# A hand-written instruction order: a transpose, one exponential and one weight step moved, and seven more matmul steps whose result is never read

## The chip, the cores and the metric

The kernel runs on one core of a Trainium2 chip. Its engines work side by side: TensorE (PE, with its weight loads as PEld), VectorE (DVE), ScalarE (ACT), GpSimd (POOL), and SyncE (SP), which here only issues DMAs. The metric is the device time of one execution in microseconds (us), as the median of three runs. Less is better.

## What is computed

Two attention steps with 32 packed rows per head, then a dense layer with a SoLU activation and a layer norm. Cut to its core:

```python
# q, k, v: (8, 8, 576, 64); p: (8, 8, 32, 64); w_in: (512, 1024); w_out: (1024, 512)
p_packed = sm_attn(p, k, v)                 # softmax(scale * p k^T) v, 32 rows per head
out = sm_attn(q, p_packed, p_packed)        # 576 rows per head
x = out.transpose(0, 2, 1, 3).reshape(4608, 512)
h = x @ w_in
solu = h * softmax(h)
ln = (solu - mean) / sqrt(var + 1e-06) * g_ln
return ln @ w_out
```

## The kernel before

For each of the 8 batches three flows prepare the data. `k0` to `k7` (`pack`) turn k, form the scores with the packed rows, take their maximum and exponential, and multiply by v: the result is the packed tile `ppT`. `q0` to `q7` (`unpack`) turn q, form the scores against `ppT`, take the softmax, and split the result into two halves of 16 bits, `a_h` and `a_l`. `z0` to `z7` (`make_z`) multiply `ppT` by w_in into Z, also split in a high and a low half. Then 36 token tiles `t0` to `t35` of 128 rows (`token_tile`) follow: 12 matmuls at each of two 512-wide halves give h (line 630), DVE, ACT and POOL make the activation, a DMA turns it, and 24 matmuls multiply by w_out (line 690).

Other flows prepare the weights: `W0` to `W3` convert w_in, `O0` to `O3` convert w_out, `C0` to `C7` scale it, `g` turns g_ln on PE (line 186) and copies it to SBUF on ACT (line 188), and `H` makes 16-bit halves of w_in for later batches: per chunk, ACT makes the high half (line 342) and DVE the low half (line 344). One step of `W0` is a pass of ACT over the chunk (line 229), a shift on DVE (line 231), and a second pass of ACT (line 242, the low bits).

`Z` and `X` compute nothing that is read. `Z` is 39 matmuls at the start. `X` (`keep_clock`) issues two matmuls of 384 columns into the spare PSUM tile each time it is called; only its columns 128 to 511 are written, and `g` uses columns 0 to 7.

Nothing here is ordered by a planner. Each flow is a Python generator, and the string `ORDER` says which flow makes its next step (line 733, `next(flows[name], None)`). Each engine takes its instructions in that order and starts one when what it waits for is there. A step that stands earlier in `ORDER` is therefore earlier on each engine's queue that it touches, and an instruction that waits holds up all that follow it on that engine. PSUM has three `h` buffers, in turn used by the transposes (lines 209, 372, 378), the first scores (line 402), the transposes of the exponentials (line 443), Z (line 576) and h.

In batch 0 the flow `k0` goes: transposes of k (372, 378), copies, scores for r = 0 (402, PE), maximum (407, DVE), exponential (410, ACT), the same three for r = 1, then the transposes of both exponentials (443, PE), of which the first needs r = 0 alone and the rest r = 1 too, then the product with v (453, PE).

Of the kernel before, what the change touches and what calls it, by code (L numbers as in the profile page):

```python
# [49 lines left out]
def packed_attention_solu_kernel(ctx: ExitStack, tc: tile.TileContext, q: bass.AP, k: bass.AP, v: bass.AP, p: bass.AP, w_in: bass.AP, w_out: bass.AP, g_ln: bass.AP, out: bass.AP):  # L50
    nc = tc.nc
    B, H, S, D = q.shape
# [67 lines left out]
        yield  # L120

    def keep_clock():
        for _ in range(4):
            for _ in range(2):
                nc.tensor.matmul(spare[:, P:], lhsT=ones, rhs=ones.unsqueeze(1).broadcast_to([P, DM // P - 1, P]), start=True, stop=True)
            yield
# [481 lines left out]
    def token_tile(i, dst, b, c):  # L608
# [77 lines left out]
        for o0 in range(0, DM, wide):  # L686
# [73 lines left out]
```

## Time and profile before

| what | before |
|---|---|
| time, median of 3 runs | 391.14 us (388.96 to 392.26) |
| the profiled execution's own time | 389.22 us |
| its span, first to last instruction | 387.4 us |
| mean granted TensorE clock | 1.000 |
| PE busy | 377.0 us (97%) |
| DVE, ACT, POOL busy | 292.5, 256.7, 245.9 us |

The span is 1.82 us shorter than the time of the same execution. The profiled execution lies near the fastest of the three runs and 1.92 us under their median. A matmul's end is modelled, so that the busy time of PE overlaps from one instruction to the next; where one group of matmuls starts after another is the safer reading.

### The profile page before, as it was taken

The page shows a single profiled execution, that of the slowest core. Times are in us where ns is not written, and L with a number is a line of the kernel's source. Part 1 is how long each engine was busy: PE and PEld are TensorE (multiplying, and loading weights), DVE is VectorE, ACT ScalarE, POOL GpSimd, SP SyncE. Part 2 cuts the span into 40 slices and gives each one's busy share as a digit, 9 for nine tenths or more (in the row PEclk, how much of TensorE's full clock was granted, in tenths as well). Part 3 has the DMA queues.
Part 4 walks back from the last instruction along what each step waited for, and adds up shares of the span by engine and source line. Part 5 has one row for each costly group of instructions (what it writes and reads, how often), then busy time and mean ns, then how long its engine had stood idle before and what let it go on. Part 6 is the DMA issues. An engine that isn't in the chain of part 4 may idle for free.

```text
span 387.4 us, 8803 instructions
## 1 busy us (share of the span) xinstructions
PE 377.0 (97%) x3380; PEld 194.6 (50%) x3380; DVE 292.5 (76%) x472; ACT 256.7 (66%) x447; POOL 245.9 (63%) x410
## 2 busy tenths in 40 slices
PE   6978999999999999999999999999999999999996
PEld 6856555444545444544454455444455444444445
DVE  2576889999997987778797589977777868477541
ACT  2386799795878677945757757754648559466640
POOL 2664589888438987764555477885456757853660
PEclk9999999999999999999999999999999999999999
DMA  8999993899899899999799878991631533344461
GB/s 304 389 374 358 205 215 57 211 187 180 153 237 171 199 197 180 173 182 219 160 191 144 215 142 175 183 179 47 159 81 37 129 91 98 85 104 104 92 162 55
DMA packets 213866, 66.11 MB, mean 171 GB/s; under 512 B 194744, under 2 KB 207808, under 8 KB 213312
## 3 DMA queue, kind: packets, MB, share of 16 engines
q1 hardware_dynamic: 213824, 65.56, 74.8%
q8 instruction: 26, 0.43, 0.5%
q14 instruction: 16, 0.13, 0.1%
HBM read 37.23 MB, written 9.44 MB: 120 GB/s over the span
## 4 chain that ended last, share of the span: by engine, by line
PE 90%; ACT 4%; DVE 2%; POOL 2%; issue 1%; DMA 1%; POOLq 0%
PE po L690 39%; PE h L630 24%; PE h L690 5%; PE h L372 4%; PE pa L453 3%; PE h L402 3%; PE h L570 2%; PE h L522 2%; PE po L117 2%; PE h L443 2%; POOL a_l L538 1%; PE po L119 1%; PE h L209 1%; PE h L576 1%; ACT e L410 1%; ACT e L672 1%
## 5 line engine op out<-in xcount | busy, mean ns | idle before, releaser
L690 PE MATMUL po<-wch,yT 128*128 128x512 f16 x512 | 160.1, 379 | 0.0
L690 PEld LDWEIGHTS <-yT 128*128 128x128 f16 x888 | 85.9, 98 | 99.2 <-issue 4.5
L690 PE MATMUL po<-wcl,yT 128*128 128x512 f16 x256 | 97.0, 379 | 0.0
L655 DVE SCALAR_TENSOR_TENSOR u<-e,s_row,h 128x1024 f32<-128x1024 f32 x36 | 45.8, 1271 | 16.5 <-ACT e L651 11.1
L633 DVE TENSOR_REDUCE nm<-h 128x1 f32<-128x1024 f32 x36 | 43.6, 1213 | 9.5 <-PE h L630 9.0
L666 DVE SCALAR_TENSOR_TENSOR yhl<-u,negmu,yhl 128x1024 f16<-128x1024 f32 x36 | 46.5, 1292 | 4.0 <-ACT yhl L664 3.9
L630 PE MATMUL h<-zh,a_h 128*128 128x512 f16 (+1 forms) x160 | 47.8, 380 | 0.0
L630 PE MATMUL h<-zl,a_h 128*128 128x512 f16 (+1 forms) x160 | 47.7, 380 | 0.0
L651 ACT ACTIVATE e<-h,nmc,z_scale 128x1024 f32<-128x1024 f32 x36 | 43.2, 1201 | 2.2 <-PE h L630 0.8
L630 PEld LDWEIGHTS <-a_h 128*128 128x128 f16 (+1 forms) x320 | 27.7, 100 | 33.0 <-issue 3.8
L664 ACT ACTIVATE yhl<-u,negmu 128x1024 f16<-128x1024 f32 x36 | 41.1, 1144 | 0.7
L672 ACT ACTIVATE e<-u,negmu 128x1024 f32<-128x1024 f32 x36 | 41.0, 1138 | 0.0
L638 ACT ACTIVATE nmc<-nm,z_scale 128x1 f32<-128x1 f32 x33 | 9.7, 293 | 44.2 <-DVE nm L633 44.1
L641 POOL TENSOR_SCALAR bound<-nm,z_scale 128x1 f32<-128x1 f32 x33 | 13.8, 419 | 36.7 <-DVE nm L633 35.3
L630 PE MATMUL h<-zl,a_l 128*128 128x512 f16 (+1 forms) x80 | 30.4, 380 | 0.4 <-POOL a_l L538 0.4
L630 PE MATMUL h<-zh,a_l 128*128 128x512 f16 (+1 forms) x80 | 30.3, 379 | 0.0
L679 POOL TENSOR_SCALAR c_row<-sq,s_eps 128x1 f32<-128x1 f32 x36 | 11.7, 326 | 28.5 <-ACT e L672 25.5
L698 DVE TENSOR_SCALAR o_sb<-po,c_row,inv 128x512 f32<-128x512 f32 x18 | 14.6, 810 | 15.8 <-PE po L690 6.9
L680 POOL TENSOR_TENSOR c_row<-c_row,neg_half 128x1 f32<-128x1 f32 x36 | 22.7, 630 | 3.0
L659 ACT ACTIVATE negmu<-su 128x1 f32<-128x1 f32 x36 | 7.2, 199 | 26.1 <-DVE u L655 26.1
L630 PEld LDWEIGHTS <-a_l 128*128 128x128 f16 (+1 forms) x160 | 14.8, 100 | 18.0 <-POOL a_l L538 1.2
L506 POOL TENSOR_TENSOR a<-a,sm 128x576 f32<-128x576 f32 x16 | 20.3, 1275 | 5.2 <-DVE sm L504 4.4
(171 smaller groups left out, 700.2 us busy)
## 6 DMA issues: line engine op xcount, KB each, us to landing
out_dram<-o_sb SPq DMA_DIRECT2D x35, 256.0 KB, 2.4
v_sb<-in_v_dram SPq DMA_DIRECT2D x8, 1024.0 KB, 7.6
raw<-in_k_dram SPq DMA_DIRECT2D x24, 288.0 KB, 4.6
raw<-in_q_dram SPq DMA_DIRECT2D x96, 72.0 KB, 2.5
zh<-in_moe_w_in_dram SPq DMA_DIRECT2D x2, 1024.0 KB, 8.4
zl<-in_moe_w_in_dram SPq DMA_DIRECT2D x2, 1024.0 KB, 9.6
raw<-in_k_dram SPq DMA_DIRECT2D x2, 1024.0 KB, 11.9
raw<-in_moe_w_out_dram SPq DMA_DIRECT2D x2, 1024.0 KB, 8.3
```

What stands on the lines that cost most here:

```text
L372: nc.tensor.matmul(pt[64 * r:64 * r + 64, g * MAIN + c * P:g * MAIN + (c + 1) * P], lhsT=rows[:, c, 2 * (g0 + g) + r], rhs=ident, start=Tr ...
L506: EN(nc, SOFT_BY[2 * b + 1]).tensor_tensor(out=w2, in0=w2, in1=sm.unsqueeze(2).broadcast_to([P, NB, J]), op=ALU.mult)
L630: nc.tensor.matmul(dst_[:, cols], lhsT=lhsT, rhs=z[:, r, cols], start=bool(first), stop=bool(last))
L633: nc.vector.tensor_reduce(out=nm, in_=h, axis=AX.X, op=ALU.max, negate=True)
L651: nc.scalar.activation(e, h, AF.Exp, bias=nmc, scale=sc[:, 1:], accum_out=se)
L655: nc.vector.scalar_tensor_tensor(out=u, in0=e, scalar=s_row, in1=h, op0=ALU.mult, op1=ALU.mult, accum_out=su)
L664: nc.scalar.activation(yhl[:, 0], u, AF.Identity, bias=negmu)
L666: nc.vector.scalar_tensor_tensor(out=yhl[:, 1], in0=u, scalar=negmu, in1=yhl[:, 0], op0=ALU.add, op1=ALU.subtract)
L672: nc.scalar.activation(e, u, AF.Square, bias=negmu, accum_out=sq)
L680: nc.gpsimd.tensor_tensor(out=c_row, in0=c_row, in1=neg_half, op=ALU.pow)
L690: nc.tensor.matmul(po[:, cols], lhsT=yT[:, a, c], rhs=w[:, c, cols], start=c == 0 and t == 0, stop=c == NFC - 1 and t == 2)
L698: nc.vector.tensor_scalar(out=o_sb[:, cols], in0=po[:, cols], scalar1=c_row, scalar2=inv, op0=ALU.mult, op1=ALU.mult)
```

## The change

Four edits, of which one also changes a function and the others only `ORDER`:

- `g` makes its first step (the transpose on PE) some 15 steps later. Its second step stays.
- `k0` makes its exponential for r = 0, its scores for r = 1 and their maximum before `W0` makes its steps, where before `W0`'s first three steps stood ahead of the exponential. The exponential for r = 1 still stands behind both ACT passes of `W0`.
- `X` is called 11 times in place of 4. Two of the new calls stand before the transposes of batch 0's exponentials; five stand between Z of batch 0 and the first token tile.
- One step of `H` (the low half of one w_in chunk, on DVE) is made seven steps later, behind the last step of batch 1's Z.

```diff
     def keep_clock():
-        for _ in range(4):
+        for _ in range(11):
             for _ in range(2):
                 nc.tensor.matmul(spare[:, P:], lhsT=ones, ...)
             yield
```

The first place in the string, cut out of its line on both sides (the same stretch before and now):

```diff
-X X k0 k0 lo1 W0 lq0 g W0 W0 k0 k0 W0 k0 p k0 k0 O0 W3 p lv0
+X X k0 k0 lo1 k0 k0 k0 W0 lq0 W0 W0 W0 p X X k0 k0 O0 W3 g p lv0
```

**PE, batch 0's first attention step.** Here `h` is a PSUM buffer, `e` in line 209 is p's rows, `e_112` the exponentials.

```order
 L378 MATMUL h<-ident,raw 128x128 x2
 L125 MATMUL po<-ones 128x384 x4
-L402 MATMUL h<-kT,pT 32x288 x8
+L402 MATMUL h<-kT,pT 32x288 x16
+L209 MATMUL h<-ident,e 64x128 x8
+L125 MATMUL po<-ones 128x384 x4
 L186 MATMUL po<-ident,g_raw 128x8
-L402 MATMUL h<-kT,pT 32x288 x8
-L209 MATMUL h<-ident,e 64x128 x8
 L443 MATMUL h<-ident,e_112 128x128 x8
```

The transpose of g no longer stands between the scores of r = 0 and r = 1, and four new unread matmuls stand right ahead of the transposes of the exponentials.

**ACT, the same place.** The rows named L229 and L242 on `zh` are the two passes of `W0`; L410 are the two exponentials.

```order
 L215 ACTIVATE pT<-h 128x512
 L380 COPY kT<-h 128x2x2x64
+L410 ACTIVATE e_112,ssum<-h,nmx 128x576
 L229 ACTIVATE e<-zh 128x1024
-L410 ACTIVATE e_112,ssum<-h,nmx 128x576
 L242 ACTIVATE u<-zh,one_up 128x1024
 L410 ACTIVATE e_112,ssum<-h,nmx 128x576
```

Only the first exponential has changed places with the first pass of `W0`; the second exponential still follows both passes.

**PE, from batch 0's Z to the first token tile** (line 630 is the first matmul of `t0`; line 372 and 378 are transposes of the next k and q, line 402 the scores of batch 1).

```order
 L576 MATMUL h<-w_in_sb,ppT 32x512 x4
+L125 MATMUL po<-ones 128x384 x2
 L372 MATMUL h<-ident,raw 64x128 x16
 L277 MATMUL pa<-ssq,ones_f 128x8
+L125 MATMUL po<-ones 128x384 x2
 L576 MATMUL h<-w_in_sb,ppT 32x512 x4
 L372 MATMUL h<-ident,raw 64x128 x16
 L576 MATMUL h<-w_in_sb,ppT 32x512 x4
+L125 MATMUL po<-ones 128x384 x2
 L378 MATMUL h<-ident,raw 128x128 x2
+L125 MATMUL po<-ones 128x384 x2
 L402 MATMUL h<-kT,pT 32x288 x8
```

Four pairs of unread matmuls are new here; a fifth pair stands after the transposes that follow, directly ahead of the first matmul of `t0`.

**DVE, batch 1's Z.** Line 344 is the step of `H`; line 586 is the low half of Z, line 666 a low half in a token tile.

```order
+L666 SCALAR_TENSOR_TENSOR yhl<-u,negmu,yhl 128x1024
+L586 SCALAR_TENSOR_TENSOR zl<-h,z_scale,zl 128x1024
 L344 SCALAR_TENSOR_TENSOR w_in_sb<-w_in_sb,s_w,w_hi 128x1024
-L666 SCALAR_TENSOR_TENSOR yhl<-u,negmu,yhl 128x1024
-L586 SCALAR_TENSOR_TENSOR zl<-h,z_scale,zl 128x1024
 L385 STREAM_TRANSPOSE kT<-raw 128x576
```

The low half of w_in now follows the other two in place of leading them. POOL's and SP's orders are the same in both kernels.

## Rows read from the trace of the kernel before

**Rows 1.** The page's busy times by engine: busy us, share, instructions.
```profile
PE 377.0 (97%) x3380; PEld 194.6 (50%) x3380; DVE 292.5 (76%) x472; ACT 256.7 (66%) x447; POOL 245.9 (63%) x410
```

**Rows 2.** Waits of PE: who waited for whom, us in total, times, longest.
```profile
PE h L209 <- DMA e<-in_p_dram: 3.0, 1, 3.0
...
PE pa L453 <- issue: 0.7, 1, 0.7
...
PE h L630 <- POOL a_l L538: 0.4, 1, 0.4
PE pa L277 <- DVE wsq L326: 0.3, 1, 0.3
```

**Rows 3.** Stretches: length, busy PE, PEld, DVE, ACT, POOL; PEclk, DMA share, GB/s.
```profile
25.00:28.00 3.00, 1.60 (x19) 1.44 (x21) 1.77 (x4) 2.55 (x6) 2.92 (x2) 1.00 1.12 355
40.00:45.00 5.00, 5.00 (x62) 2.86 (x60) 4.90 (x12) 3.13 (x5) 3.46 (x3) 1.00 1.00 257
45.00:50.00 5.00, 4.42 (x58) 2.56 (x58) 3.86 (x13) 4.41 (x10) 3.17 (x3) 1.00 1.07 170
50.00:55.00 5.00, 5.00 (x86) 3.79 (x80) 4.33 (x8) 5.00 (x9) 4.18 (x4) 1.00 1.08 271
200.00:300.00 100.00, 100.00 (x946) 49.27 (x945) 79.15 (x129) 66.43 (x120) 62.38 (x111) 1.00 0.67 138
```

**Rows 4.** Timeline of DVE and ACT, batch 0's exponentials: start, busy, idle before.
```profile
22.33 0.76 DVE L407 TENSOR_REDUCE nmx<-h 128x1 f32<-128x576 f32 x1 [0.76 <-PE h L402]
...
22.04 1.18 ACT L229 ACTIVATE e<-zh 128x1024 f32<-128x1024 f32 x1 [1.03 <-DMA zh<-in_moe_w_in_dram]
23.12 0.74 ACT L410 ACTIVATE e<-h,nmx 128x576 f32<-128x576 f32 x1
...
23.85 1.24 ACT L242 ACTIVATE u<-zh,one_up 128x1024 int32<-128x1024 uint32 x1
25.51 0.74 ACT L410 ACTIVATE e<-h,nmx 128x576 f32<-128x576 f32 x1 [0.42 <-DVE nmx L407]
```

**Rows 5.** Timeline of PE, the start and batch 0's exponentials.
```profile
2.97 1.97 PE L209 MATMUL h<-ident,e 128*64 128x128 f32 x16 [2.97 <-DMA e<-in_p_dram]
...
23.46 1.09 PE L209 MATMUL h<-ident,e 128*64 128x128 f32 x16
...
26.39 0.98 PE L443 MATMUL h<-ident,e 128*128 128x128 f32 x7 [1.58 <-ACT e L410]
```

**Rows 6.** Timeline of PE in short windows: one and four unread matmuls.
```profile
39.62 0.44 PE L125 MATMUL po<-ones 128*128 128x384 f32 x1
...
39.62 0.98 PE L125 MATMUL po<-ones 128*128 128x384 f32 x4
```

**Rows 7.** Timeline of PE, from batch 0's Z to the first token tile.
```profile
47.17 1.06 PE L576 MATMUL h<-w_in_sb,ppT 64*32 64x512 f32 x8
48.35 0.44 PE L378 MATMUL h<-ident,raw 128*128 128x128 f32 x2
49.25 1.20 PE L402 MATMUL h<-kT,pT 64*32 64x288 f32 x16 [0.46 <-ACT kT L380]
...
55.30 0.60 PE L630 MATMUL h<-zh,a_h 128*128 128x512 f16 x2
```

**Rows 8.** Timeline of POOL and DVE, batch 1's Z and low halves.
```profile
88.44 1.26 POOL L682 TENSOR_SCALAR c_row<-c_row,inv 128x1 f32<-128x1 f32 x1
89.66 2.25 POOL L538 TENSOR_TENSOR a_l<-s,a_h 128x576 f16<-128x576 f32 x1
...
91.87 1.27 POOL L538 TENSOR_TENSOR a_l<-s,a_h 128x576 f16<-128x576 f32 x1
...
88.31 1.25 DVE L344 SCALAR_TENSOR_TENSOR w_in_sb<-w_in_sb,s_w,w_hi 128x1024 f16<-128x1024 f32 x1
89.48 1.29 DVE L666 SCALAR_TENSOR_TENSOR yhl<-u,negmu,yhl 128x1024 f16<-128x1024 f32 x1
90.69 1.27 DVE L586 SCALAR_TENSOR_TENSOR zl<-h,z_scale,zl 128x1024 f16<-128x1024 f32 x1
```

More of the change, by code (lines that the diff above doesn't have):

```diff
@@ new lines @@
+ORDER = 'lp lw2 lw3 lw1 W2 W2 W3 lk0 W2 lo0 lp p W3 W3 Z k0 lw0 k0 W3 lg W2 W1 W1 k0 k0 O0 k0 W1 p k0 W2 X X k0 k0 lo1 k0 k0 k0 W0 lq0 W0 W0 W0 p X X k0 k0 O0 W3 g p lv0 k0 k0 O1 p W1 q0 lo2 k0 W1 O0 k0 q0 O1 O1 q0 k0 O0 W0 q0 k0 q0 O0 O1 lo3 q0 p k0 k0 k0 p k0 k0 g O2 q0 O2 k0 N q0 N O2 z0 q0 p q0 lk1 q0 q0 z0 X X q0 O3 O1 q0 O2 z0 X k1 lk2 lq1 S X z0 O2 q0 z0 q0 z0 z0 O3 q0 z0 lk2 q0 k1 q0 k1 z0 X z0 S q0 q0 k1 q0 k1 X k1 S k1 q0 q0 C2 z0 q0 z0 k1 z0 O3 O3 q0 q0 q1 k1 C2 C3 H lk2 C4 q1 q0 q0 k1 C2 C5 O3 C5 k1 C4 lk2 q0 C3 q1 X t0 C6 k2 k1 k2 C4 k1 t0 C0 q1 t0 t0 t1 C3 k2 k1 k1 k2 k1 t1 lv1 C5 t0 C0 k1 t0 lk3 t0 C6 q1 k1 t1 lk3 k1 C0 t2 k1 t1 t0 q1 k1 t2 C1 k1 C7 t1 q1 k1 q1 q1 lq2 C7 t3 t1 t0 C1 t0 C6 C1 q1 t3 t2 t2 C7 k1 q1 q1 lk3 q1 t0 k2 lv2 t0 k1 k2 t0 t1 t3 k2 t0 t1 z1 t2 t1 t1 q1 t3 q1 t0 q1 t2 t0 t0 lk3 t2 z1 t3 q2 t2 z1 t2 H q1 z1 z1 k2 t3 t1 q1 lq3 H t1 t1 q1 k2 t2 t1 q1 q1 H q1 t1 z1 k2 k2 k2 t1 t3 lq2 k2 q1 z1 t2 k2 k3 q1 t1 q1 t2 q1 lq2 lq2 t2 t2 t2 z1 k2 q1 t2 t3 z1 H q1 t4 k3 q2 t2 t4 q2 H t3 t5 t5 k2 k2 H t3 q2 t3 t4 t4 lk4 t5 t5 t3 k2 lq3 k2 t4 t3 t4 k2 t5 lq3 k2 t4 t5 k2 k2 q2 H t4 q2 q2 q2 z2 t6 t5 t4 lk4 q2 H t3 q2 t4 z2 t6 t4 t3 q2 z2 z2 t6 t3 z2 t4 t5 t4 t6 k3 k3 z2 k3 lv3 t6 t3 q2 t5 k3 t6 t6 k3 lq3 t5 t5 k3 t4 z2 t4 lk4 t6 lk4 k3 t6 q2 t7 q2 t4 k3 k3 q2 t7 q3 q3 t6 k3 z2 k3 t7 q2 t5 q3 t7 t5 k3 q2 k3 t5 q2 t5 k3 q2 k3 t4 t5 t7 t5 t8 t8 q2 z2 z2 q2 t7 k3 t6 q3 q2 t7 k4 z2 k4 q2 t8 k3 q2 t6 t7 t6 q2 k4 k4 t6 t6 q2 z2 t8 lv4 k3 t6 q3 t8 q3 k4 lk5 z2 q3 k3 q3 k3 k4 t7 q3 t8 t9 t8 q3 t6 t7 lq4 t8 lk5 k3 q3 t8 lk6 t9 t10 k4 t8 q3 t7 z3 z3 t10 q3 t7 t7 q3 t9 lk5 t9 t10 t10 t9 t9 t7 t7 z3 t9 z3 t8 z3 t10 k4 t7 t7 t8 q3 t9 q3 t8 lk5 z3 t9 t10 q3 t8 z3 k4 t8 q3 t10 t10 z3 q4 t8 q3 q3 t11 t11 z3 k4 z3 z3 lq4 t9 t11 q3 t11 k5 t9 k4 k4 t12 k4 q3 q4 t8 t11 z3 t10 k5 lq4 t10 t9 t9 t9 k5 t11 k4 t9 k5 lk6 k4 q3 lq4 lk6 z3 t11 t9 t12 q3 k4 t11 k4 t10 t9 t12 k4 q3 q3 lk7 t12 k5 t11 q4 t10 k4 t10 k5 k4 t10 t10 q4 q4 t12 t12 k5 lq5 q4 q4 q4 t10 q4 lk6 t10 t12 t11 q4 k5 t13 k4 q4 t11 t13 t12 lv5 k5 t13 q4 t15 t11 t13 t13 t11 t13 t11 q4 t12 t13 q4 t13 t11 q4 t11 t11 k5 k6 q4 t15 t14 lk7 q4 lq5 t12 t13 t14 t12 t12 t15 t15 t12 t14 t13 t15 t12 k5 t13 t15 t12 t16 t14 k4 t12 t14 t12 t13 t13 t13 k6 t13 lk7 t14 t14 q4 t15 t16 t14 lk7 k4 q5 k5 t17 t14 t13 k6 t13 q4 lq5 t14 q4 q4 t15 k6 t14 k5 lq5 k5 t16 k5 t17 q4 z4 q4 t16 t14 t14 k5 k5 q4 t15 q4 t17 q5 t15 z4 t16 t17 z4 t14 t16 q5 k5 t16 t14 t17 t14 z4 z4 t15 t16 k6 k5 q5 k5 q4 k5 t15 t17 lq6 t14 z4 t16 t17 t15 k6 t15 z4 k5 k5 z4 z4 z4 q5 q5 k6 z4 z4 k6 q5 t16 q5 k6 t15 t15 k6 lv6 q5 t17 z4 t18 t18 t18 t19 k6 t16 t18 q5 t16 q5 z5 q5 t18 t15 t16 q5 t19 t16 t17 lq6 q5 t17 t16 t19 lq6 t18 q6 lq6 t16 t19 t18 t20 k6 t20 t19 t18 t19 q5 t17 z5 t17 t16 t17 q6 k6 z5 lq7 t19 q5 k6 t18 t17 t17 t20 t18 lq7 t20 q5 k6 q6 t19 t17 z5 t20 t18 z5 t20 q5 k6 t17 k6 q5 t19 lv7 t20 z5 q5 t21 k7 q5 t19 t21 z5 q5 k7 k7 t19 t21 q5 k6 q5 t18 t18 t18 q5 t18 t20 t19 q6 t21 z5 k6 t19 z5 t18 t19 t21 q5 t19 k6 t18 lq7 z5 t21 z5 q6 k7 t20 t21 z5 t19 k6 q6 q6 z5 k7 k7 t20 t22 k7 t19 t22 t21 t21 k7 q6 t20 t20 t20 t22 k7 t21 k7 t23 t20 q6 q6 q6 q6 t22 t20 t23 t22 q6 t22 q7 q6 q6 k6 q7 t22 t20 t21 t22 t23 t20 t21 lq7 t22 t23 t22 t21 t21 t23 t23 k6 t21 t21 z6 t24 t23 q6 t22 t24 z6 t23 t22 t21 q6 t22 t24 q6 t23 t22 k7 t22 t22 q6 t22 k7 q6 t24 t23 t24 t24 t24 q6 q6 t25 k7 q6 t24 z6 t25 t24 t23 t25 t23 t23 t23 t23 t23 k7 t25 t24 t23 k7 q6 t25 t25 t26 t26 t24 k7 k7 t25 t26 k7 z6 q6 t26 t26 t25 q6 z6 z6 q7 z6 t26 t24 k7 z6 t24 z6 q7 z6 t25 t24 z6 t24 z6 k7 z6 t24 t24 q7 k7 q7 q7 q7 t27 t26 q7 t27 q7 k7 t26 t27 t26 t25 t25 q7 t25 t25 t25 k7 z7 q7 t27 t25 t28 z7 q7 t27 t26 t25 z7 t25 t27 t28 t27 t26 t26 t26 t28 t27 t26 t26 t27 t28 q7 t29 t29 t28 t28 t26 z7 t28 t28 q7 t27 q7 t26 t27 t28 t29 z7 t29 q7 t29 z7 q7 t27 t27 t28 t27 t27 q7 t28 q7 q7 z7 t29 t27 t29 t29 q7 z7 z7 t28 q7 q7 z7 t27 t28 z7 t29 t28 z7 q7 t29 t28 q7 t28 z7 t30 t30 t31 t30 t30 t29 t31 t30 t29 t29 t32 t31 t30 t30 t28 t30 t29 t31 t31 t29 t30 t30 t30 t32 t33 t29 t30 t30 t31 t31 t31 t30 t30 t32 t33 t29 t32 t32 t32 t31 t32 t30 t30 t34 t31 t33 t31 t32 t34 t32 t33 t34 t31 t31 t31 t32 t31 t34 t33 t31 t33 t33 t32 t33 t31 t35 t34 t32 t35 t34 t34 t32 t33 t35 t33 t32 t33 t32 t34 t35 t32 t33 t33 t34 t33 t35 t34 t35 t35 t35 t32 t33 t35 t34 t33 t34 t33 t34 t35 t34 t35 t35 t35 t35 t34 t34 t34 t35 t35 t35 t35 t35'
```

1 line of the change is left out of this document (removed).

## The prediction

> **What bounds the kernel now.** I read the page first: PE is busy 377.0 of 387.4 us, and no other engine comes near it [rows 1]. Then I asked where PE waits. The list of its waits has seven rows, 7.0 us in all, and all but one lie before the first token tile: 3.0 us for the first DMA, 1.58 us for batch 0's second exponential [rows 5], 0.7 us with no releaser before the last part of the product with v, and three short ones. The only later one is 0.4 us for POOL's low half of batch 1's a [rows 2]. So from 55.30 us, where `t0` starts [rows 7], PE streams: in 200 to 300 us it is busy 100 of 100 us [rows 3]. The kernel is a lead-in of 55.3 us and then a stretch in which PE has next to no slack. What the change does to the time is therefore read from two questions: when does `t0` start, and does the one later wait go or grow?
>
> The stretches of the lead-in tell where there is room. PE is busy 1.60 of 3.00 us in 25 to 28, but 5.00 of 5.00 in 40 to 45, 4.42 in 45 to 50 and 5.00 in 50 to 55 [rows 3]. Unread matmuls are free in the first of these and are paid in the others, but for the holes of 45 to 50.
>
> **g turned later.** One small matmul leaves the place between the scores of r = 0 and r = 1 and comes behind the new unread ones, in PE's wait of 1.58 us [rows 5]. The second step, on ACT, has not moved, so nobody waits longer for it. I take 0. Bounds: nothing to gain but the matmul's own fraction of a 0.1 us, and nothing to lose as long as the wait covers it.
>
> **The first exponential sooner.** The exponential for r = 0 can't start before its maximum is done. That is at 22.33 + 0.76 = 23.09 us, and in the kernel before it started at 23.12 us, right behind the first pass of `W0` [rows 4]. So this pass cost it nothing: it stood in a gap in which ACT would have waited for the maximum. Now ACT idles in that gap, and the pass comes behind the exponential. What PE waits for is the second exponential, for r = 1 [rows 5], and that still follows both passes. From the starts: the pass takes 23.12 − 22.04 = 1.08 us of ACT, the exponential 23.85 − 23.12 = 0.73 us, and the second pass 1.24 us less the same overlap of 0.10 us, 1.14 us. The second exponential is now free to start at 23.12 + 0.73 + 1.08 + 1.14 = 26.07 us, against 25.51 us before, 0.56 us later. The maximum for r = 1 is earlier than before, but it no longer ends the wait. Behind the exponential stand seven of the eight transposes, the copy of the result and the product with v, all of which PE takes one after another. So +0.56 us, unless the 0.7 us wait with no releaser ahead of the product's end [rows 2] is a fixed point in time that eats it: then 0. I take +0.56, since the chain between is PE's own, and keep 0 as the other end.
>
> **Seven more unread steps.** A step is two matmuls. One alone is shown as 0.44 us, four as 0.98 [rows 6]: each further one adds (0.98 − 0.44)/3 = 0.18 us, so a step takes 0.36 us of PE's stream.
> - Two steps stand ahead of the transposes of the exponentials. Before, PE idled there for 1.58 us [rows 5], and in the change for 0.56 us more; 0.72 us of matmuls are hidden. Without that cover they would cost 0.72 us.
> - Steps 3 and 4 stand between Z and transposes within 40 to 45 us, where PE has no hole [rows 3]: +0.72 us.
> - Step 5 stands between the last product of Z and the transposes at 48.35 us. Z's eight records begin at 47.17 us and are shown for 1.06 us, thus to 48.23; about 0.1 us of that is the modelled end, so the hole is some 0.22 us wide and 0.36 − 0.22 = +0.14 us is paid.
> - Step 6 stands ahead of the scores of batch 1, which waited 0.46 us for a copy on ACT [rows 7]: hidden, 0. That copy follows PE's own transposes, so it moves with them.
> - Step 7 stands directly ahead of `t0`, in a full stretch [rows 3]: +0.36 us.
>
> Together 0.72 + 0.14 + 0.36 = +1.22 us. The bounds are 0, if other engines set the start of `t0` and PE's shown busy time hides slack, and 7 × 0.36 = 2.52 us, if nothing is covered. ACT is just as full as PE in 50 to 55 us (5.00 of 5.00), which is what speaks for the lower end; but its work there follows PE's transposes, and so shifts with them.
>
> **The low half of w_in.** Before, POOL's small step at 88.44 us is shown for 1.26 us and the first `a_l` for 2.25 us, against 1.27 us for the second [rows 8]. Both long ones end about when a DVE instruction with two SBUF operands ends: line 344 (88.31 to 89.56 us) and line 666 (89.48 to 90.77 us). PE's 0.4 us wait ends on the second `a_l`, at 91.87 + 1.27 = 93.14 us. With line 344 out of the way, line 666 comes first and takes its place as the blocker of the small step; line 586, which reads PSUM, follows at 89.5 us; the first `a_l` then runs from about 89.75 to 91.02 us, unhindered. If the second follows directly it ends at 92.3 us and the 0.4 us wait is gone. If line 344, due on DVE at 90.7 us, comes between, the second `a_l` waits its 1.2 us and ends at about 93.5 us: 0.4 us worse. By the rows alone the edit is worth −0.4 us. The Trainium skill (SBUF — State Buffer, Who interferes with whom) says that a VectorE instruction with two SBUF inputs and a GpSimd one that reads SBUF exclude each other for a whole instruction, and that issue order decides who blocks. The trace agrees (2.25 against 1.27 us). By that rule the conflict is not removed but moved to the next pair, and the sum would be 391.4 in place of 390.6. I take 0, the middle, and both ends for the range.
>
> **The sum.** 389.22 + 0.56 + 1.22 + 0 = 391.0 us. It is made against the profiled execution, 1.92 us under the median of the runs shown; their spread of 3.3 us is larger than any term. I forecast that the change's median lands where its profile does, at 391.0, level with the median before.
>
> **Rivals.**
> *All hidden.* The wait with no releaser eats the 0.56 us, the new matmuls fall into slack that the modelled ends conceal, and the 0.4 us wait goes: 389.22 + 0 to 0.6 − 0.4, so 388.8 to 389.9, say 389.3. For it: other engines are nearly full too. Against it: 10 us of PE at 100% [rows 3].
> *The runs' spread stays on top.* What lifted two of three runs by 2 to 3 us before is not in this profile. If it remains, the median is 391.0 + 1.9 = 392.9.
> *Slower: PE's clock.* The first 16 records of line 209 take 1.97 us, the same 16 later 1.09 us [rows 5], while the granted clock is printed as 1.00 everywhere [rows 3]: after idling, PE starts at the lower of its two levels. The wait at 24.8 us is now up to 0.56 us longer, less 0.72 us of matmuls. Should the clock fall there to 1.2 GHz, each us of PE's work costs 0.81 us more (1.97/1.09); 395.05 us, 1% above before, is reached when 4.05/0.81 = 5 us of the work between 27 and 55 us are done so. Against it: PE's wait as a whole is no longer than before. The Trainium skill (TensorE: Matmul & The Clock Gate, Part 1) calls the lower clock the default that activity lifts; by that rule the unread steps could as well take off the 1.9 us of spread, which is the difference between the forecast and the rival above.
> *Faster by over 1%*, under 387.2: needs all of PE's lead-in waits after the first, 3.6 us, to vanish, and nothing of the new steps to be paid.
>
> **How the numbers follow.** Forecast (390.2 to 391.8) 0.50; all hidden (388.8 to 390.2) 0.22; spread stays (391.8 to 395.0) 0.20; slower 0.05; faster 0.03. The range for 8 in 10 is 388.8 to 393.6: it holds the forecast, the hidden case and most of the third. About 1% is what a measurement of this kernel tells from no change; only the last two cases cross it, so faster 0.03, same 0.92, slower 0.05.
>
> **What would show it.** Right: the second exponential at 26.1 us and PE's wait for it to near 26.95; `t0` at 55.30 + 1.78 = 57.1 us; no other wait of PE between Z and `t0` than before, the one of 0.46 us shrunk to 0.1. Wrong: `t0` at 55.3 or before (hidden), a row of line 209, 372 or 443 lasting near twice its time before (clock), or PE's wait for `a_l` past 0.8 us (line 344 between the two).

## The result, and the profile after

The changed kernel takes 392.82 us (median of 19 runs, 392.01 to 393.25), the kernel before, run beside it, 389.35 us (19 runs, 387.39 to 392.26). The ratio is 1.0085, with a 95% interval from 1.0071 to 1.0098: the change costs 3.5 us. The forecast was 391.0 us, read as no move from a median of 391.14.

The profiled execution took 392.85 us with a span of 391.1 us, 3.7 us more than before. PE's waits show first where to look (line waited for: us in total, times, longest).

```profile
PE h L443 <- ACT e L410: 2.4, 2, 2.2
...
PE h L522 <- ACT wch L305: 0.5, 1, 0.5
PE pa L468 <- ACT squares L466: 0.5, 1, 0.5
PE h L630 <- DVE u L655: 0.4, 1, 0.4
...
PE po L690 <- DMA yT<-yhl: 0.2, 1, 0.2
PE h L378 <- ACT e1T L445: 0.2, 1, 0.2
PE h L402 <- DVE u L655: 0.2, 1, 0.2
```

Against [rows 2], the 0.7 us without a releaser and the 0.4 us for `a_l` are gone. Six lines with short waits are new, and line 443 has a second wait of 0.2 us; all of these waits lie behind `t0` and end between 63.9 and 115.9 us. The stretches of after say the same, in order of time (length, busy PE, PEld, DVE, ACT, POOL; PEclk, DMA share, GB/s).

```profile
25.00:28.00 3.00, 1.88 (x17) 1.72 (x19) 1.67 (x4) 2.97 (x7) 2.37 (x1) 0.87 1.12 360
28.00:30.00 2.00, 2.00 (x24) 2.00 (x22) 0.35 (x1) 0.84 (x1) 1.50 (x1) 0.50 1.13 278
...
60.00:70.00 10.00, 8.95 (x134) 5.01 (x132) 9.38 (x15) 8.26 (x16) 7.91 (x11) 1.00 0.19 32
...
100.00:110.00 10.00, 9.29 (x142) 4.70 (x131) 9.50 (x20) 7.90 (x15) 3.84 (x11) 1.00 0.87 158
110.00:120.00 10.00, 9.68 (x113) 4.18 (x112) 9.05 (x12) 7.21 (x13) 3.75 (x9) 1.00 1.15 236
...
200.00:300.00 100.00, 100.00 (x945) 49.27 (x944) 79.18 (x130) 63.45 (x117) 62.69 (x113) 1.00 0.64 145
```

The same stretches of before, behind `t0`:

```profile
60.00:70.00 10.00, 10.00 (x151) 4.92 (x150) 9.17 (x18) 8.78 (x19) 9.57 (x11) 1.00 0.55 104
...
100.00:110.00 10.00, 10.00 (x118) 4.56 (x117) 9.93 (x21) 7.33 (x15) 3.77 (x9) 1.00 0.86 170
110.00:120.00 10.00, 10.00 (x78) 5.06 (x77) 6.97 (x12) 8.82 (x16) 5.30 (x11) 1.00 0.97 199
```

PE was full here before. Now it loses 1.05 us in 60 to 70, and 0.71 + 0.32 = 1.03 us in 100 to 120. Far behind, in 200 to 300, PE is as full as in [rows 3].

The lead-in, as the timelines of after show it (start, length, engine, line): first ACT, which answers [rows 4],

```profile
22.38 0.74 ACT L410 ACTIVATE e<-h,nmx 128x576 f32<-128x576 f32 x1 [2.11 <-DVE nmx L407]
...
23.11 1.12 ACT L229 ACTIVATE e<-zh 128x1024 f32<-128x1024 f32 x1
24.14 1.21 ACT L242 ACTIVATE u<-zh,one_up 128x1024 int32<-128x1024 uint32 x1
25.26 0.72 ACT L410 ACTIVATE e<-h,nmx 128x576 f32<-128x576 f32 x1
```

then PE, which answers [rows 5, 7].

```profile
20.05 1.52 PE L402 MATMUL h<-kT,pT 64*32 64x288 f32 x32 [0.55 <-ACT pT L215]
...
26.12 0.98 PE L443 MATMUL h<-ident,e 128*128 128x128 f32 x7 [2.22 <-ACT e L410]
27.03 1.84 PE L209 MATMUL h<-ident,e 128*64 128x128 f32 x16
...
40.90 0.69 PE L513 MATMUL h<-qT,ppT 64*32 64x288 f32 x8
...
42.38 0.62 PE L125 MATMUL po<-ones 128*128 128x384 f32 x2
42.92 1.97 PE L372 MATMUL h<-ident,raw 128*64 128x128 f32 x32
...
45.06 0.60 PE L125 MATMUL po<-ones 128*128 128x384 f32 x2
45.60 1.06 PE L576 MATMUL h<-w_in_sb,ppT 64*32 64x512 f32 x8
...
56.83 0.62 PE L125 MATMUL po<-ones 128*128 128x384 f32 x2
57.29 0.61 PE L630 MATMUL h<-zh,a_h 128*128 128x512 f16 x2
```

`t0` starts at 57.29 us, 1.99 us later than in [rows 7]. Of this 1.66 us arises between line 513 and `t0` (57.29 − 40.90 = 16.39 us); the kernel before has line 513 here,

```profile
40.57 0.69 PE L513 MATMUL h<-qT,ppT 64*32 64x288 f32 x8
```

and so 55.30 − 40.57 = 14.73 us. All in all: 0.33 us up to line 513, 1.66 us to `t0`, 1.05 and 1.03 us of new waits, less the 0.4 us wait that went. That is 3.67 us, the difference of the two spans. So 2.08 us of new waits lie behind `t0`, 1.7 us net of the one that went, where the change moves nothing but one step of `H`.

**What happens there.** VectorE's low half of `t0` (line 666, 128x1024) and POOL's subtraction for a low half of w_out (line 313, 128x512) start within some 0.1 us of each other. Line 633 is DVE's maximum of `t0`'s h, and line 641 is POOL's small step that reads it. Before, on DVE and POOL:

```profile
58.10 1.23 DVE L633 TENSOR_REDUCE nm<-h 128x1 f32<-128x1024 f32 x1
...
64.31 1.28 DVE L666 SCALAR_TENSOR_TENSOR yhl<-u,negmu,yhl 128x1024 f16<-128x1024 f32 x1
...
59.51 0.31 POOL L641 TENSOR_SCALAR bound<-nm,z_scale 128x1 f32<-128x1 f32 x1
...
64.41 2.20 POOL L313 TENSOR_TENSOR wcl<-yT,wch 128x512 f16<-128x512 f32 x1
```

After:

```profile
60.09 1.23 DVE L633 TENSOR_REDUCE nm<-h 128x1 f32<-128x1024 f32 x1 [0.53 <-PE h L630]
...
66.31 2.29 DVE L666 SCALAR_TENSOR_TENSOR yhl<-u,negmu,yhl 128x1024 f16<-128x1024 f32 x1
...
61.43 0.31 POOL L641 TENSOR_SCALAR bound<-nm,z_scale 128x1 f32<-128x1 f32 x1 [0.47 <-DVE nm L633]
...
66.36 1.16 POOL L313 TENSOR_TENSOR wcl<-yT,wch 128x512 f16<-128x512 f32 x1
```

Before, POOL is the one that is held up (2.20 us), and PE has no wait in 60 to 70 us. After, it is DVE (2.29 us), and what follows on DVE is a full 1.0 us late. That is the copy of `ppT` (line 462, at 68.52 us), which line 522 on PE reads (the list puts its wait down to ACT's line 305, which ends 0.06 us later; in a kernel below it names line 462), and then `u` (line 655, at 68.72 us), for which line 630 on PE waits 0.4 us. The recorded starts, 0.10 us apart before and 0.05 us after, name DVE as first in both; the lengths tell who was. The Trainium skill (SBUF — State Buffer, Who interferes with whom) says that such a pair excludes each other for a whole instruction and that issue order decides who blocks. The trace agrees, with 2.29 against 1.28 us on DVE and 2.20 against 1.16 us on POOL.

### The profile page after: what moved, and what is told of

It reads as the page before. It is cut to its first block, busy times and chain, and to the rows that moved or that the text cites. A ratio compares the mean times of both kernels' runs of the same rounds, so it can differ in the third digit from the quotient of the medians.

```text
span 391.1 us, 8831 instructions
## 1 busy us (share of the span) xinstructions
PE 379.4 (97%) x3394; PEld 197.5 (51%) x3394; DVE 294.2 (75%) x472; ACT 256.6 (66%) x447; POOL 244.1 (62%) x410
## 4 chain that ended last, share of the span: by engine, by line
PE 82%; DVE 8%; ACT 5%; issue 1%; DMA 1%; POOL 1%; SPq 0%; DVEq 0%
PE po L690 37%; PE h L630 21%; PE h L690 5%; PE h L372 4%; PE h L402 3%; PE h L570 2%; PE po L117 2%; PE h L522 2%; PE pa L453 2%; DVE nm L633 1%; PE h L443 1%; DVE u L655 1%; PE h L209 1%; PE h L576 1%; DVE w_in_sb L344 1%
## 5 line engine op out<-in xcount | busy, mean ns | idle before, releaser
L666 DVE SCALAR_TENSOR_TENSOR yhl<-u,negmu,yhl 128x1024 f16<-128x1024 f32 x36 | 48.5, 1348 | 4.0 <-ACT yhl L664 3.9
L679 POOL TENSOR_SCALAR c_row<-sq,s_eps 128x1 f32<-128x1 f32 x36 | 12.7, 352 | 28.9 <-ACT e L672 26.0
```

The costliest lines, as they stand in the source:

```text
L666: nc.vector.scalar_tensor_tensor(out=yhl[:, 1], in0=u, scalar=negmu, in1=yhl[:, 0], op0=ALU.add, op1=ALU.subtract)
```

## The experiments

The theory after the result: the late steps turn this order, and the turned order, not the steps' own length, is the loss behind `t0`. The rivals: the clock that falls near 28 us; the work of the new steps itself; the moved step of `H`. In all diffs `X` is one unread step, and each difference is between a median and that of the kernel before, run beside it (389.2 to 389.4 us each time); two kernels are compared by these differences.

**The parts, one at a time.** The five late steps alone, on the kernel before:

```diff
-O2 z0 k1 lk2 lq1 S z0 ... k1 z0 z0 S q0 q0 k1 q0 k1 k1 S ... C3 q1 t0 C6
+O2 z0 X k1 lk2 lq1 S X z0 ... k1 z0 X z0 S q0 q0 k1 q0 k1 X k1 S ... C3 q1 X t0 C6
```

> The kernel before with only the five late unread steps (two between Z of batch 0 and the transposes, two around the transposes at 48 us, one ahead of the first token tile). In the profile of the change a late step took 0.46 to 0.54 us from its start to the next instruction's, not 0.36, and the first token tile came 1.66 us later measured from there. Theory 1 (the steps move the first token tile against POOL's queue, so that a POOL subtraction of line 313 starts before the DVE low half of line 666 near 66 us and holds it up by 1.0 us): t0 1.6 to 1.7 us later, that line 666 shown for 2.3 us in place of 1.28, in all 2.6 to 3.0 us slower than before. Theory 2 (only PE's stream counts): 1.6 to 1.7 us slower, line 666 at 1.28 us.

Measured: 393.86 us, ratio 1.0139 [1.0112, 1.0167], 4.7 us over before. Line 666 takes 2.27 us, as the theory says, but the loss is larger than its 2.6 to 3.0 us; what the rest is, the kernels with `H` moved and not moved show below.

g, the first exponential and the two early steps alone:

```diff
-X X k0 k0 lo1 W0 lq0 g W0 W0 k0 k0 W0 k0 p k0 k0 O0 W3 p lv0
+X X k0 k0 lo1 k0 k0 k0 W0 lq0 W0 W0 W0 p X X k0 k0 O0 W3 g p lv0
```

> The kernel before with only the first stretch changed: g later, the first exponential ahead of W0, two unread steps ahead of the transposes of the exponentials. Theory 1: the second exponential, which starts behind both passes of W0, is 0.5 us later relative to the scores; the clock falls to 1.2 GHz near 27.6 us as in the change (granted clock 0.5 for some 2 to 3 us) and costs up to 1.4 us of PE, part of it taken from the 0.7 us wait in the product with v: 0.5 to 1.4 us slower in the lead-in, with the port order near 66 us open. Theory 2 (the wait in the product eats it, clock as before): 0 to 0.2 us slower.

Measured: 389.83 us, ratio 1.0015 [0.9999, 1.0032], 0.6 us over before, between the two theories. The granted clock falls here as in the changed kernel (0.77 in 25 to 30 us), line 666 stays at 1.28 us, and by the interval the time is at most 1.3 us more. So the clock is at most a small part of the loss. The 19 runs of the change say the same: the six with a mean granted clock of 0.999 or 1.000 have a median of 392.6 us, the 13 with 0.996 one of 392.9 us.

The step of `H` alone (it moves by five places in `ORDER`, not by seven):

```diff
-t2 z1 H k2 q1 t2 t3 z1 q1
+t2 z1 k2 q1 t2 t3 z1 H q1
```

> The kernel before with only the step of H moved behind batch 1's Z. Theory 1: the wait of 0.4 us for the low half of a at 93 us goes, nothing else: 0.2 to 0.4 us faster. Theory 2 (DVE and POOL meet at another pair, as in the change, where line 666 near 91 us took 2.3 us): DVE is 1 us late from there on, full as it is, and PE waits near 100 to 115 us: 0.3 to 0.8 us slower.

Measured: 389.66 us, ratio 1.0015 [0.9993, 1.0037]: no difference that the runs tell from none, so neither theory is borne out. The profiled execution, at 392.5 us, was one of the two longest of the twelve.

The change without its last unread step, the one directly ahead of `t0`:

```diff
-q0 C3 q1 X t0 C6 k2
+q0 C3 q1 t0 C6 k2
```

> The change without its last unread step, the one directly ahead of the first token tile. Theory 1: t0 is 0.46 us earlier, POOL is no longer ahead, line 666 near 66 us takes 1.28 us again and blocks POOL instead: 1.4 to 1.6 us faster than the change. Theory 2 (the step costs its own time alone): 0.4 to 0.5 us faster than the change.

Measured: 390.45 us, ratio 1.0036 [1.0024, 1.0048]. A step of 0.46 us (57.29 − 56.83) is taken away and 2.2 us go with it (3.5 less 1.3), more than the 1.4 to 1.6 us expected. Line 666 and line 313 are back to their old order:

```profile
65.87 1.28 DVE L666 SCALAR_TENSOR_TENSOR yhl<-u,negmu,yhl 128x1024 f16<-128x1024 f32 x1
...
65.99 2.18 POOL L313 TENSOR_TENSOR wcl<-yT,wch 128x512 f16<-128x512 f32 x1
```

**That step alone, on the kernel before.** Is it the sum of the late steps, or the place of this one?

```diff
-q0 C3 q1 t0 C6 k2
+q0 C3 q1 X t0 C6 k2
```

> The kernel before with one unread step alone, the one directly ahead of the first tile. If this step's place is what turns the order of line 666 and POOL's line 313: line 666 takes 2.3 us and the time is 391 to 392 us. If it is the sum of the late steps that counts (POOL's lead of some 0.4 us at the first tile, which one step of 0.46 us may just not use up, since the delay reaches POOL too): line 666 stays at 1.28 us and the time is 389.3 + 0.46 = 389.8 us.

Measured: 392.41 us, ratio 1.008 [1.0064, 1.0096], just above the 391 to 392 us of the first case. One step of 0.46 us (55.43 to 55.89 us) costs 3.1 us, nearly what the whole change does. It is the place, and not how late `t0` is: the other four late steps without it bring `t0` to 56.86 us, and the order stays; this one alone brings it to 55.89 us, and the order turns. In the profile with only the step of `H` moved, a fall of the clock puts `t0` at 58.61 us, and there too the order stays (line 666 at 1.27 us). DVE and POOL of the kernel with the one step:

```profile
58.69 1.23 DVE L633 TENSOR_REDUCE nm<-h 128x1 f32<-128x1024 f32 x1 [0.55 <-PE h L630]
...
64.90 2.28 DVE L666 SCALAR_TENSOR_TENSOR yhl<-u,negmu,yhl 128x1024 f16<-128x1024 f32 x1
...
60.03 0.31 POOL L641 TENSOR_SCALAR bound<-nm,z_scale 128x1 f32<-128x1 f32 x1 [0.49 <-DVE nm L633]
...
64.94 1.15 POOL L313 TENSOR_TENSOR wcl<-yT,wch 128x512 f16<-128x512 f32 x1
```

The 3.1 us are not made up as the 3.5 us are. This kernel has a wait behind line 586 that the change, with `H` moved, does not have,

```profile
PE h L630 <- DVE zl L586: 1.5, 1, 1.5
```

and it has no loss in 100 to 110 us, where the change loses 0.71 us.

The chain is read off here. All other late steps stand ahead of transposes, on which the copies of ACT and DVE depend, so that delay reaches every engine. This one stands behind all of them and delays the matmuls of `t0` alone. Line 633 on DVE, which used to start behind DVE's own work, now waits 0.55 us for them. POOL's line 641, which used to start late because POOL was still busy with its own line 313 (58.24 to 59.39 us before), now waits 0.49 us for line 633. From line 633 to line 641 it is 59.51 − 58.10 = 1.41 us before and 60.03 − 58.69 = 1.34 us here. From line 633 to line 666, and from line 641 to line 313, the distances are the same in both (6.21 us, and 4.90 against 4.91 us). POOL has thus gained 0.07 us on DVE, and that turns the order.

| kernel | line 633 waits for PE | 633 to 641 | line 666 | line 313 | time over before |
|---|---|---|---|---|---|
| before | no | 1.41 | 1.28 | 2.20 | – |
| early edits alone | no | 1.41 | 1.28 | 2.19 | 0.6 |
| change without last step | no | 1.41 | 1.28 | 2.18 | 1.3 |
| last step alone | 0.55 | 1.34 | 2.28 | 1.15 | 3.1 |
| the change | 0.53 | 1.34 | 2.29 | 1.16 | 3.5 |
| five late steps | 0.54 | 1.34 | 2.27 | 1.15 | 4.7 |

**The order turned by other means.** If 0.07 us decide, the order can be set without touching PE. In the changed kernel POOL is held back by two fills that nobody reads (`Y` is the new flow; its entry in the table of flows is left out here and below):

```diff
+    def pool_pad():
+        t = const.tile([P, P], F32, name='pad')
+        for _ in range(2):
+            nc.gpsimd.memset(t, 0.0)
+        yield
-lk3 k1 C0 t2 k1
+lk3 k1 Y C0 t2 k1
```

> The change with two unread POOL fills of 128x128 ahead of the one POOL subtraction of line 313 that starts near 66 us (0.3 to 0.4 us of POOL; PE's and DVE's orders untouched, all unread matmul steps kept). Theory 1 (who starts first on that pair decides): line 666 near 66 us takes 1.28 us again, line 313 is the one that is held up, PE's waits of 0.5 and 0.4 us near 69 us and those near 100 to 120 us go: 1.5 to 2.2 us faster than the change, though POOL got more work. Theory 2 (the change's loss beyond the start of the first tile comes from elsewhere): as the change, within 0.4 us.

Measured: 391.26 us, ratio 1.0034 [1.0007, 1.0062]. Work is added and 1.5 us are won against the change (3.5 less 1.9); line 633 waits as long as in the change (0.55 us), so the wait itself does little harm. The stretches of this kernel behind `t0`:

```profile
60.00:70.00 10.00, 9.81 (x138) 5.39 (x137) 8.84 (x16) 9.10 (x19) 8.92 (x14) 1.00 0.27 50
...
100.00:110.00 10.00, 10.00 (x150) 5.37 (x147) 9.87 (x21) 7.79 (x15) 3.92 (x11) 1.00 0.95 167
110.00:120.00 10.00, 10.00 (x115) 4.26 (x114) 7.74 (x10) 8.12 (x14) 4.37 (x10) 1.00 1.00 221
```

Of the 1.05 us in 60 to 70 us 0.2 us stay, a wait of line 378 that does not hang on the order; the other losses behind `t0` are gone. Its line 666 and line 313:

```profile
66.65 1.28 DVE L666 SCALAR_TENSOR_TENSOR yhl<-u,negmu,yhl 128x1024 f16<-128x1024 f32 x1
...
67.09 1.86 POOL L313 TENSOR_TENSOR wcl<-yT,wch 128x512 f16<-128x512 f32 x1
```

The reverse, on the kernel before: DVE is held back by an instruction of one column ahead of line 666.

```diff
+    def pad():
+        t = const.tile([P, P], F32, name='pad')
+        nc.vector.tensor_scalar_max(t[:, :1], neg_half, 2.0 ** (-60))
+        yield
-C0 t2 k1 t1 t0 q1
+C0 t2 k1 t1 Y t0 q1
```

> The kernel before with one VectorE instruction of one column, read by nobody, ahead of the first tile's second low half (line 666, the eighth step of t0); it writes to a tile of 512 bytes per partition, so that other tiles keep their alignment, which the same edit with a 4-byte tile did not. Order-flip theory: line 666 now comes to the shared pair behind POOL's line 313, takes 2.2 to 2.3 us in place of 1.28, PE waits near 69 us and again between 100 and 120, and the time is 390.5 to 393 us (before: 389.3), for 0.1 us of added work. Rival, the loss comes from PE's late steps themselves and the flip is only seen beside it: line 666 may take 2.3 us but the time stays within 0.5 us of before. Third, the instruction is too short to change the order: line 666 stays at 1.28 us and the time at 389.3 us.

Measured: 391.23 us, ratio 1.0051 [1.0026, 1.0077]. Line 666 starts 6.28 us behind line 633 (63.77 − 57.49), in place of 6.21, and is now the one held up:

```profile
63.71 0.14 DVE L705 TENSOR_SCALAR pad<-neg_half 128x1 f32<-128x1 f32 x1
63.77 2.28 DVE L666 SCALAR_TENSOR_TENSOR yhl<-u,negmu,yhl 128x1024 f16<-128x1024 f32 x1
...
63.81 1.15 POOL L313 TENSOR_TENSOR wcl<-yT,wch 128x512 f16<-128x512 f32 x1
```

PE's work is untouched here, and 0.07 us on DVE cost 1.9 us. In 60 to 70 us PE is busy 9.05 us, a loss of 0.95 us, near that of the change. The profile also has a wait of 1.4 us for a turned activation (line 690, at 81 us), which the change does not have, so the size does not carry over one to one. A tile of 512 bytes without a turned order was run only in the changed kernel above, where it cost nothing that shows. So the turned order is a cause by itself.

**The step of `H` once DVE is late.** The change with this step back at its old place:

```diff
-t2 z1 k2 q1 t2 t3 z1 H q1
+t2 z1 H k2 q1 t2 t3 z1 q1
```

> The change with the step of H back where it was. Theory 1 (where DVE is 1 us late, line 344 and line 666 are both held up by POOL's low halves, as in the run with the five late steps alone, where PE waited 1.5 us for batch 1's Z): 0.8 to 1.2 us slower than the change. Theory 2 (the place of H is worth nothing either way): within 0.3 us of the change.

Measured: 394.13 us, ratio 1.0116 [1.0060, 1.0173], 1.3 us more than the change; all six runs lie above all 19 of the change. Both low halves near 92 us are now blocked, each by a POOL line 538,

```profile
91.60 2.29 DVE L344 SCALAR_TENSOR_TENSOR w_in_sb<-w_in_sb,s_w,w_hi 128x1024 f16<-128x1024 f32 x1
93.81 2.29 DVE L666 SCALAR_TENSOR_TENSOR yhl<-u,negmu,yhl 128x1024 f16<-128x1024 f32 x1
```

and PE waits 1.5 us for line 586 behind them. In the change only line 666 is blocked there (91.33 us, 2.30 us). So the edit that is worth nothing on the kernel before is worth 1.3 us once DVE has lost its lead. The account then reads: 4.7 us for the five late steps and 0.6 for the early edits, less 1.3 for `H`, are 4.0 us, against 3.5 measured. The intervals leave room for the rest.

**Both exponentials ahead of `W0`.** The second exponential is what PE waits for, so does PE win when it comes sooner?

```diff
-X X k0 k0 lo1 W0 lq0 g W0 W0 k0 k0 W0 k0 p k0 k0 O0 W3 p lv0
+X X k0 k0 lo1 k0 k0 k0 k0 k0 W0 lq0 g W0 W0 W0 p O0 W3 p lv0
```

> The kernel before with both exponentials of batch 0 ahead of W0's steps (four unread steps as before, g and H as before). If the second exponential is what bounds PE near 26 us, the transposes of the exponentials start 1.6 to 2.1 us earlier relative to the scores, and t0 does too unless a transfer (v or q) or W0's later conversion ends the wait then: 1.0 to 2.0 us faster than before where nothing else is late, 0 to 0.5 us if the wait goes to a DMA. The order of line 666 and line 313 near 66 us could flip; then 2 us of it are lost again.

Measured: 390.3 us, ratio 1.0003 [0.9974, 1.0032]. The seven transposes of line 443 come 3.92 us behind the start of the scores in place of 5.59, and nothing of that is left in the time. PE's waits of this kernel:

```profile
PE h L372 <- ACT pT L215: 2.1, 1, 2.1
PE pa L453 <- issue: 1.6, 1, 1.6
```

The product with v, line 453, is held to nearly the same distance from the issue of the last part of v as before: its last part starts at 34.89 us here and at 34.25 us before, 12.0 and 11.7 us behind that issue (22.92 and 22.53 us). The likely releaser is that DMA; the trace names none, so this is argued and not shown.

**A small tile.** The same DVE instruction with a tile of 4 bytes per partition:

```diff
+        t = const.tile([P, 1], F32, name='pad')
+        nc.vector.tensor_scalar_max(t, neg_half, 2.0 ** (-60))
```

> The kernel before with one unread DVE instruction on 128x1 (about 0.2 us) directly ahead of line 666 near 64 us, and nothing else. Theory 1: line 313 on POOL now starts first, line 666 takes 2.3 us, PE waits near 67 us and again behind 88 us, where line 344 and line 666 are held up too: 2.0 to 3.0 us slower than before for 0.2 us of added work. Theory 2: within 0.3 us of before.

Measured: 400.25 us, ratio 1.0266 [1.0216, 1.0316]. The loss of 10.9 us is far above the 2 to 3 us expected. Line 666 did turn (2.30 us), but PE also waited 4.8 us for the DMAs that turn the activation, so the loss can't be put down to the order. Two controls without the DVE instruction, with a fill of the tile on POOL, first 4 and then 32 bytes per partition:

```diff
+        t = const.tile([P, 1], F32, name='pad')
+        nc.gpsimd.memset(t, 0.0)
```

> The kernel before with one tile of 4 bytes per partition allocated at the same place, and one POOL fill of it (read by nobody), no VectorE instruction. Address theory: the DMAs that turn the activation (yT from yhl) land later than in the kernel before (4.7 in place of 4.0 us), PE waits for them 4 to 5 us in all, and the time is 396 to 401 us. Rival, the 11 us of the earlier kernel came from the VectorE instruction and its order alone: then the DMAs land as before and the time is 389 to 391 us.

> The kernel before with one tile of 32 bytes per partition (in place of the 4 bytes of the run before) and the same POOL fill of it, read by nobody. If it is the alignment of the tiles behind it that counts, and 32 bytes keep it, the DMAs that turn the activation land in 4.0 us as in the kernel before and the time is 389 to 390 us. If 32 bytes are not enough, or if it is the fill and not the address, the DMAs land in 4.5 us and the time is 396 to 400 us, as with 4 bytes. The order of line 666 and POOL's line 313 near 64 us should be that of before (1.28 and 2.2 us).

Measured: 399.44 us, ratio 1.0243 [1.0222, 1.0264], and 398.81 us, ratio 1.0264 [1.0188, 1.0341]. Line 666 keeps its 1.28 us in both. The DMA views say what grew (tiles, queue, count, median us from issue to landing), here before and then with 4 bytes:

```profile
yT<-yhl SPq DMA_TRANSPOSE x36, 4.0
```

```profile
yT<-yhl SPq DMA_TRANSPOSE x36, 4.5
```

It is 4.5 us with 32 bytes too ([P, 8] in place of [P, 1]), and 4.0 us with the 512 bytes of the kernel above. The plain loads land later as well: in the same views the 96 loads of q take 2.9 us with 4 and with 32 bytes, against 2.5 us before. The kernel with 4 bytes and a DVE instruction differs from the one with 512 bytes in the tile's size alone and takes 9.0 us more. So the small tile costs 9 to 10 us, and 32 bytes are no better than 4. Two fills of a 512-byte tile cost nothing that shows in the kernel above, so it is not the fill. That it does so by the addresses of the tiles that lie behind it is argued and not shown: no view shows an address.

## Why the prediction was wrong, point by point

- **What bounds the kernel: right, and not used to its end.** PE streams from `t0` on, so each new wait behind `t0` is paid in full. But the text asked only when `t0` starts and what becomes of the one later wait. It never asked which engines would still keep their distance to PE. `t0` came at 57.29 us, where 57.1 was forecast, and the time was missed all the same: nearly half of the loss lies behind `t0`.
- **The step that failed** is the term for new waits behind `t0`, which the sum has at nothing. The nearest it comes to a ground is the sentence on ACT, whose work "follows PE's transposes, and so shifts with them"; DVE and POOL were not asked about. As far as the order of DVE and POOL goes, this holds for steps 3 to 6 (without step 7 the order stays) and fails for step 7, which stands behind the last transpose. Step 7 was priced at 0.36 us; alone it costs 3.1 us, and in the change 2.2 us hang on it. In place of nothing the profile has 2.08 us of new waits, less the 0.4 us that went. The pair that turned, line 666 and line 313, stood in the trace of before with its 2.20 us on POOL and 0.10 us between the starts. The same conflict was weighed for `H` near 89 us [rows 8] and not looked for behind `t0`.
- **Unread steps, the size: 1.22 us forecast, 1.66 measured.** The price of 0.36 us came from the spacing of further matmuls in a row of four [rows 6]. A pair of its own between other work takes 42.92 − 42.38 = 0.54, 45.60 − 45.06 = 0.54 and 57.29 − 56.83 = 0.46 us from its start to the next one's. That the first matmul of a row is shown as 0.44 us was in the same row.
- **The first exponential: right where it was read, and then partly hidden.** The transposes that wait for the second exponential came 6.07 us (26.12 − 20.05) behind the start of the scores, against 5.59 before: +0.48, forecast 0.56. Up to line 513 only 0.33 us of all that comes ahead of it is left, since the 0.7 us without a releaser went. The forecast named this wait as the lower end, "a fixed point in time that eats it", and took the other end; the kernel with both exponentials sooner bears the fixed point out.
- **The start of `t0` at 57.29 us is in part luck.** In this execution the scores began 0.75 us sooner (20.05 against 20.80 us), because the unread matmuls at the start (line 117) took 6.51 in place of 7.25 us; over the profiles of all kernels they take 6.45 to 7.67 us, whatever the edit. That gain, the clock, the wait that went and the longer steps, none of them in the sum, came out near its 1.78 us together.
- **The clock.** It did fall, at the place named: 0.87 in 25 to 28 and 0.50, the lower level, in 28 to 30 us, and the 16 records of line 209 take 1.84 us in place of 1.09. PE had waited 2.22 us just before, against 1.58 us [rows 5]. It is no fixed result of the edits: the change with `H` at its old place has the same lead-in and a wait of 2.2 us, and its clock stays at 1.00 in 25 to 35 us. From the start of line 209 to the last two transposes of line 443 it is 31.47 − 27.03 = 4.44 us, against 30.16 − 27.31 = 2.85 us before, so the fall takes 1.6 us. It costs little, because the wait ahead of line 453 takes most of it up: the early edits with the same fall are 0.6 us over before.
- **g: 0, as far as the runs tell it,** since it was only run together with the other early edits.
- **The low half of w_in: 0 forecast, and 0 alone.** The wait for `a_l` is still 0.4 us there, so neither of the two ends came true. In the change the move is worth −1.3 us, because of the late DVE, which the forecast did not have.
- **The base.** The sum of 391.0 us was made against 389.22 us and then called level with a median of 391.14. Over 19 runs the median is 389.35 us: the profile stood for the kernel, and the three runs shown did not. Read so, the same sum was a forecast of +1.8 us. Of the 3.5 us, this leaves 1.7 us to explain, and the order of line 666 and line 313 explains it: turned back, it gives 1.5 us. The rival that gave 392.9 us, a spread of the runs that stays on top, met the number by luck: the 19 runs lie within 1.3 us.
- The range of 388.8 to 393.6 us holds the result. The change stays within 1%, as forecast.

None of the kernels tried is faster than the one before.

## What to carry to other kernels

When a change delays one engine, ask for each other engine whether the same delay reaches it; those that it doesn't reach can change their order on whatever they share. In the trace of before, look for instructions that take nearly twice their usual time: here those looked at marked a pair that is decided by its order, and the gap between the two starts tells how little turns it. And put unread work, if at all, ahead of something on which all engines depend, not directly ahead of the stage that is the bound.

## What the runs showed of the hardware

- A pair of VectorE and POOL on SBUF is turned by 0.06 to 0.07 us. In the kernels looked at, DVE was first when POOL's recorded start was 0.10 us or more behind its own, and POOL was first when it was 0.04 to 0.06 us behind. The start that is recorded is thus not the moment that decides.
- One more tile of 4 or of 32 bytes per partition in the pool `const` costs 10 us, with the transposing DMAs at 4.5 in place of 4.0 us and the loads of q at 2.9 in place of 2.5 us; 512 bytes cost nothing of this kind. The Trainium skill (DMA: Bandwidth & Descriptors, DMA Transpose (X-bar), Constraints) asks for 32-byte alignment of a transposing DMA. A tile of 32 bytes was no better than one of 4 (398.81 and 399.44 us); no view shows the addresses, so whether the alignment is the cause, and of which tile, stays open.
- The granted clock can fall in the lead-in with no edit near it: the profile of the kernel with only the step of `H` moved has 0.78 in 40 to 55 us, where that of before has 1.00. None of the profiles with the late steps shows a fall there; whether they prevent it was not settled, and at the median they cost more than they save.
